# Larger VectorE steps, less work around the softmax, and a corner of wq loaded by four GpSimd DMAs

## The chip, the cores and the metric

One core of a Trainium2 chip runs the whole program. The metric is the device time of one execution in microseconds (us). Three executions of the kernel before took 1305.59, 1305.48 and 1307.32 us, median 1305.59 us. Weights, caches and activations lie in device memory (HBM); the core has 16 DMA engines that bring them into its on-chip memory (SBUF, 128 partitions), TensorE (PE) for matmuls into PSUM, VectorE (DVE), ScalarE (ACT), GpSimd (POOL) and SyncE (SP), which here only issues DMAs.

## The reference

A decode step of a transformer block, in float32, for 4 sequences (B) with one new token each, D = 512, H = 32 heads of Dh = 128, a cache of S = 4096 positions, F = 1792:

```python
xn = layernorm(x)
q = (xn @ wq) as [B, H, 1, Dh]
p = softmax((q . k_cache) * Dh ** -0.5)          # k_cache [B, H, S, Dh]
attention = (p . v_cache) as [B, 1, H*Dh] @ wo   # v_cache [B, H, S, Dh]
ffn = silu(xn @ w1) @ w2
out = x + attention + ffn
```

The two caches are 268 MB each, the weights wq and wo 8.4 MB each, w1 and w2 3.7 MB each. Every byte of them is read once.

## The kernel before

The work is cut into T = 32 tiles. One tile is one sequence and a group of G = 4 heads; its K and its V are 8.4 MB each, 64 KB in each of the 128 partitions: 32 partitions to a head, R = 128 positions to a partition. K tiles have two buffers (`kpool`, name `k_t`), V tiles one (`vpool`, name `v_t`). SP issues all loads in program order on one queue: w1, x, wq, K0, K1, and then V(i), K(i+2) in turn; the last V goes into a K buffer, and wo (two pieces) and w2 (four pieces of 7, 4, 2 and 1 rows of 2 KB a partition) come behind it. A load is issued when its buffer is free: for V(i) that is when the matmuls of V(i-1) are done, for K(i+2) when VectorE is done with K(i). The buffers of w1 and x (`scratch`) and wq (`wq_t`) are the first K buffer and the V buffer, so K1 waits for the feed-forward's first half and V0 for the projection of the queries.

Ahead of the tiles: layer norm on VectorE, `xn @ w1` and SiLU, `xn @ wq`, and a spread of q over partitions (`q_h`); `queries(n)` then makes, per four tiles, with four matmuls of 32 partitions, a copy of each head's q in all of the head's partitions.

For each tile, `products` multiplies K by q on VectorE (`STEP` = 32 positions at a time) and GpSimd adds the upper half of the products to the lower (`POOL_ROWS` positions, at the last step `POOL_ROWS_LAST`); `sums` reduces them on VectorE to scores; `maxima` finds a head's largest score; `softmax` on ScalarE writes exp(scale * s - scale * max) to `p_t`. `values` multiplies p by V on TensorE into `o_ps` (32 matmuls of 512 columns in four column groups), and `heads_out` takes from `o_ps` the block that belongs to each head: a ScalarE copy to `o_sb`, a VectorE multiplication by `own`, a VectorE reduction, and one matmul into `o_all`.

Behind the last tile: `heads_out` of tile 31, the division by the softmax sums (`o_row`), a transposition by matmuls (`ot`), the products with wo and the first 7 rows of w2 into `part`, a copy, the rest of w2 and the sums into `acc`, a copy to `res`, and four small stores. The order on each engine is that of the program as the scheduler leaves it; what a line waits for is set by the tiles it reads and writes.

Of the kernel before, what the change touches and what calls it, by code (L numbers as in the profile page):

```python
# [8 lines left out]
F32 = mybir.dt.float32  # L9
AF = mybir.ActivationFunctionType  # L10
ALU = mybir.AluOpType
AX = mybir.AxisListType.X

EPS = 1e-5
G = 4
STEP = 32
POOL_ROWS = 32
POOL_ROWS_LAST = 16
WO_CUTS = (16,)
W2_CUTS = (7, 11, 13)  # L20

# [2 lines left out]
def kernel(  # L24
# [23 lines left out]
    nc = tc.nc  # L48
    P = nc.NUM_PARTITIONS
    B, H, S, Dh = k_cache.shape  # L50
# [3 lines left out]
    FC = F // P  # L54
    FT = 4

    FN = [(FC + 3 - j) // 4 for j in range(4)]
    F0 = [sum(FN[:j]) for j in range(4)]
    PH = P // G
    R = S * G // P  # L60
    T = H // G * B
    NR = 4
    half = Dh // 2
    scale = float(Dh) ** -0.5
# [3 lines left out]
    const = ctx.enter_context(tc.tile_pool(name="const", bufs=1))  # L68
    kpool = ctx.enter_context(tc.tile_pool(name="kpool", bufs=2))
    vpool = ctx.enter_context(tc.tile_pool(name="vpool", bufs=1))  # L70
    small = ctx.enter_context(tc.tile_pool(name="small", bufs=2))
# [4 lines left out]
    def load_tile(pool, name, cache, i):  # L76
        t = pool.tile([P, R, Dh], F32, name=name)
        h, b = i // B * G, i % B
        src = cache[b, h : h + G].rearrange("h s d -> (h s) d")
        nc.sync.dma_start(t, src.rearrange("(p r) d -> p r d", p=P))  # L80
        return t
# [8 lines left out]
    nc.sync.dma_start(w1_t, w1.rearrange("(p c) f -> p c f", p=P))  # L90
    nc.sync.dma_start(x_sb, xf)
    wq_t = vpool.tile([P, R, Dh], F32, name="v_t").rearrange("p (c m) d -> p c (m d)", c=DC)
    nc.sync.dma_start(wq_t, wq.rearrange("(p c) n -> p c n", p=P))
    ks = {0: load_tile(kpool, "k_t", k_cache, 0)}


    const.tile([P, 48], F32, name="fill")
    ident = const.tile([P, P], F32, name="ident")
    make_identity(nc, ident)
    ones = const.tile([P, 1], F32, name="ones")  # L100
# [3 lines left out]
    p_t = const.tile([P, R, G], F32, name="p_t")  # L104
# [4 lines left out]
    m_t = const.tile([P, PH], F32, name="m_t")  # L109
# [13 lines left out]
    o_ps = ps_1.tile([P, NR * Dh], F32, name="o_ps")  # L123
    nc.vector.memset(o_ps, 0.0)
    acc = ps_1.tile([P, P], F32, name="acc")
    nc.vector.memset(acc, 0.0)
    o_all = ps_1.tile([H, B, Dh], F32, name="o_all")
    nc.tensor.matmul(
        o_all.rearrange("h b d -> h (b d)"), w_t[:, :H], p_t.rearrange("p r g -> p (r g)"),
        start=True, stop=False,  # L130
# [6 lines left out]
        axis=AX, op=ALU.add,  # L137
# [4 lines left out]
    own = const.tile([P, NR], F32, name="own")  # L142
# [4 lines left out]
    def accumulate(lhsT, rhs, start=False, stop=False):  # L147

        for j in range(D // P):
            nc.tensor.matmul(  # L150
                acc[32 * j : 32 * j + B, :], lhsT, rhs[:, j * P : (j + 1) * P],
                start=start, stop=stop,
            )

    accumulate(ident[:B, :B], x_sb, start=True)


# [32 lines left out]
    for c in range(DC):  # L190
        for j in range(4):
# [4 lines left out]
                start=(c == 0), stop=(c == DC - 1),  # L196
            )
    for j in range(4):
        rows, n = slice(32 * j, 32 * j + B), FN[j] * P
        nc.scalar.activation(h_sb[rows, :n], hp[rows, :n], AF.Silu)  # L200
    ht_ps = ps_s.tile([P, FT, 4, B], F32, name="sm")
    for t in range(FT):
# [3 lines left out]
            ident.rearrange("p (j m) -> p j m", j=4)[:, :, :B],  # L206
            start=True, stop=True,
        )
    ht_sb = const.tile([P, FT, 4, B], F32, name="ht_sb")
    nc.vector.tensor_copy(ht_sb, ht_ps)  # L210
    hT = [ht_sb[:, t, j, :] for j in range(4) for t in range(FN[j])]


    NM = H // G // 4
    qp = ps_s.tile([P, G * Dh], F32, name="sm")
    for m in range(NM):
        for c in range(DC):
            for j in range(4):
                n = NM * j + m
                a = PH - B - B * m  # L220
# [4 lines left out]
                    start=(m == 0 and c == 0),  # L225
                    stop=(m == NM - 1 and c == DC - 1),
# [5 lines left out]
    qh_ps = ps_q.tile([P, B, Dh], F32, name="q_ps")  # L232
    for b in range(B):
        for g in range(G):
# [4 lines left out]
                start=True, stop=True,  # L239
            )  # L240
    q_h = const.tile([P, B, Dh], F32, name="q_h")
    nc.vector.tensor_copy(q_h, qh_ps)  # L242

    q_ps, vs, st = {}, {}, {}

    def queries(n):

        t = ps_q.tile([P, B, Dh], F32, name="q_ps")
        for g in range(G):
            rows = slice(g * PH, (g + 1) * PH)  # L250
            k = g * PH + PH // 4 * (n // NM) + n % NM
            nc.tensor.matmul(  # L252
                t[rows].rearrange("p b d -> p (b d)"),
                ident[rows, k : k + 1].to_broadcast([PH, PH]),
                q_h[rows].rearrange("h b d -> h (b d)"),
                start=True, stop=True,
            )
        for b in range(B):
            q_ps[n * B + b] = t[:, b, :]

    def products(i, a):

        k, q = ks[i], q_ps[i]
        if a == 0:
            st[i] = small.tile([P, R], F32, name="s")
        z = a + STEP
        nc.vector.tensor_tensor(  # L267
            k[:, a:z, :], k[:, a:z, :], q[:, None, :].to_broadcast([P, STEP, Dh]), op=ALU.mult
        )
        v = a + halved(a)  # L270
        nc.gpsimd.tensor_tensor(  # L271
            k[:, a:v, :half], k[:, a:v, :half], k[:, a:v, half:], op=ALU.add
        )

    def halved(a):
        return POOL_ROWS if a + STEP < R else POOL_ROWS_LAST

    def sums(i, a):
        k, s = ks[i], st[i]
        v, z = a + halved(a), a + STEP  # L280
        if v < z:
            nc.vector.tensor_reduce(s[:, v:z], k[:, v:z, :], axis=AX, op=ALU.add)  # L282
        nc.vector.tensor_reduce(s[:, a:v], k[:, a:v, :half], axis=AX, op=ALU.add)  # L283

    def maxima(i):

        nc.vector.tensor_reduce(m_t[:, :1], st[i], axis=AX, op=ALU.max)  # L287
        mt = small.tile([P, PH], F32, name="mt", bufs=1)
        nc.vector.transpose(mt, m_t)
        gm = small.tile([P, 1], F32, name="gm", bufs=1)  # L290
        nc.vector.tensor_reduce(gm, mt, axis=AX, op=ALU.max)
        mb = small.tile([P, PH], F32, name="mb", bufs=1)
        nc.vector.tensor_scalar_mul(mb, gm.to_broadcast([P, PH]), -scale)
        nb = small.tile([P, PH], F32, name="nb", bufs=1)
        return nb, nc.vector.transpose(nb, mb).ins  # L295

    def softmax(i, nb):
        s = st.pop(i)
        for g in range(G):
            rows = slice(g * PH, (g + 1) * PH)  # L300
            nc.scalar.activation(  # L301
                p_t[rows, :, g], s[rows, :], AF.Exp, bias=nb[rows, :1], scale=scale,
                accum_out=l_t[rows, i % B, i // B, g : g + 1],
            )

# [15 lines left out]
    def heads_out(i):  # L321

        h, b = i // B * G, i % B
        o_sb = small.tile([P, NR, Dh], F32, name="o_sb", bufs=1)
        nc.scalar.activation(  # L325
            o_sb.rearrange("p r d -> p (r d)"), o_ps, AF.Copy
        )
        nc.vector.tensor_tensor(  # L328
            o_sb, o_sb, own[:, :, None].to_broadcast([P, NR, Dh]), op=ALU.mult
        )  # L330
        o_1 = small.tile([P, Dh], F32, name="o_1", bufs=1)
        nc.vector.tensor_reduce(o_1, o_sb.rearrange("p r d -> p d r"), axis=AX, op=ALU.add)  # L332
        nc.tensor.matmul(  # L333
            o_all[:, b, :], w_t[:, W0 - h : W0 - h + H], o_1, start=False, stop=(i == T - 1)
        )

    queries(0)
    ks[1] = load_tile(kpool, "k_t", k_cache, 1)
    nb = done = None
    for i in range(T):  # L340
# [12 lines left out]
        else:  # L353
            vs[i] = load_tile(kpool, "k_t", v_cache, i)
        for a in range(STEP, R, STEP):
            products(i, a)
            sums(i, a - STEP)
        sums(i, R - STEP)
        del ks[i], q_ps[i]
        nb, done = maxima(i)  # L360
# [5 lines left out]
    w2_t = kpool.tile([P, R, Dh], F32, name="k_t").rearrange("p r d -> p (r d)")  # L366
    w2_t = w2_t[:, : FC * D].rearrange("p (f n) -> p f n", f=FC)
    for t, w, n, cuts in ((wo_t, wo, H, WO_CUTS), (w2_t, w2, FC, W2_CUTS)):
        w = w.rearrange("(p f) n -> p f n", p=P)
        edges = (0, *cuts, n)  # L370
        for a, z in zip(edges[:-1], edges[1:]):
            nc.sync.dma_start(t[:, a:z, :], w[:, a:z, :])

    softmax(T - 1, nb)
    values(T - 1)
    heads_out(T - 1)


    ls_ps = ps_s.tile([H, B], F32, name="sm")
    for b in range(B):  # L380
        nc.tensor.matmul(
            ls_ps[:, b : b + 1], l_t[:, b].rearrange("p n g -> p (n g)"), ones,
            start=True, stop=True,
        )
    rl = const.tile([H, B], F32, name="rl")
    nc.vector.reciprocal(rl, ls_ps)
    o_row = const.tile([H, B, Dh], F32, name="o_row")
    nc.vector.tensor_tensor(
        o_row, o_all, rl[:, :, None].to_broadcast([H, B, Dh]), op=ALU.mult
    )  # L390
# [1 line left out]
    for n in range(NQ):  # L392
        nc.tensor.matmul(  # L393
            ot_ps, up[:, NQ - 1 - n : NQ - 1 - n + P], o_row[:, :, n * H : (n + 1) * H],
            start=(n == 0), stop=(n == NQ - 1),
        )
    ot = const.tile([P, H, B], F32, name="ot")
    nc.vector.tensor_copy(ot, ot_ps.rearrange("p b c -> p c b"))  # L398

    part = ps_q.tile([P, D], F32, name="q_ps")  # L400
    nc.vector.memset(part, 0.0)
    rows = [(ot[:, c, :], wo_t[:, c, :]) for c in range(H)]
    rows += [(hT[f], w2_t[:, f, :]) for f in range(W2_CUTS[0])]
    for c, (a, w) in enumerate(rows):
        j = 32 * (c % 4)
        nc.tensor.matmul(  # L406
# [3 lines left out]
    nc.scalar.activation(part_sb, part, AF.Copy)  # L410
    accumulate(pick[:, :B], part_sb)
    for f in range(W2_CUTS[0], FC):
        accumulate(hT[f], w2_t[:, f, :], stop=(f == FC - 1))

    res = small.tile([P, P], F32, name="s")
    nc.vector.tensor_copy(res, acc)  # L416
    for j in range(D // P):
        eng = nc.sync if j % 2 == 0 else nc.scalar
# [33 lines left out]
```

## Time and profile before

| what | us |
|---|---|
| median of three executions | 1305.59 |
| profiled execution, its time | 1305.64 |
| profiled execution, its span (first to last instruction) | 1303.9 |
| PE busy | 356.0 |
| VectorE busy | 973.8 |
| ScalarE busy | 92.7 |
| GpSimd busy | 511.2 |
| HBM read | 561.00 MB, 430 GB/s over the span |

The span is 1.74 us shorter than the execution's own time; that remainder lies outside the instructions. Times below count from the first instruction. A DMA that is spread over the 16 engines leaves sixteen landing events in the trace, one for each engine; from the first to the last of them one reads how far the engines have drifted apart. A packet record of the trace has its queue, start, duration and size; here a packet of 64 KB is one partition's row of one tile.

### The profile page before, as it was taken

The page shows a single profiled execution, that of the slowest core. Times are in us where ns is not written, and L with a number is a line of the kernel's source. Part 1 is how long each engine was busy: PE and PEld are TensorE (multiplying, and loading weights), DVE is VectorE, ACT ScalarE, POOL GpSimd, SP SyncE. Part 2 cuts the span into 40 slices and gives each one's busy share as a digit, 9 for nine tenths or more (in the row PEclk, how much of TensorE's full clock was granted, in tenths as well). Part 3 has the DMA queues.
Part 4 walks back from the last instruction along what each step waited for, and adds up shares of the span by engine and source line. Part 5 has one row for each costly group of instructions (what it writes and reads, how often), then busy time and mean ns, then how long its engine had stood idle before and what let it go on. Part 6 is the DMA issues. An engine that isn't in the chain of part 4 may idle for free.

```text
span 1303.9 us, 6301 instructions
## 1 busy us (share of the span) xinstructions
PE 356.0 (27%) x2484; PEld 88.1 (7%) x2484; DVE 973.8 (75%) x540; ACT 92.7 (7%) x297; POOL 511.2 (39%) x142
## 2 busy tenths in 40 slices
PE   4221223321222321133232033222113333112327
PEld 1000000000000000000000000000000000000002
DVE  1499777887777797777797777788777779777770
ACT  1010000000000000000000000000000000000000
POOL 0255333444333444332444433344433344433340
PEclk9755666655666665666665666665566665556668
DMA  9999999999999999999999999999999999999997
GB/s 402 449 420 447 422 445 424 443 426 442 427 439 431 436 433 434 434 433 435 435 431 439 430 437 430 439 428 441 426 438 429 438 429 440 427 442 427 441 423 330
DMA packets 10437, 561.40 MB, mean 431 GB/s; under 512 B 1172, under 2 KB 1188, under 8 KB 1448
## 3 DMA queue, kind: packets, MB, share of 16 engines
q1 hardware_dynamic: 10392, 561.01, 99.4%
q8 instruction: 19, 0.31, 0.1%
q14 instruction: 10, 0.08, 0.0%
q10 hardware_dynamic: 16, 0.00, 0.0%
HBM read 561.00 MB, written 0.01 MB: 430 GB/s over the span
## 4 chain that ended last, share of the span: by engine, by line
DMA 71%; PE 23%; another core or an unknown queue 4%; issue 2%; DVE 0%; ACT 0%; SPq 0%; ACTq 0%
DMA v_t<-in_A_v_cache_dram 65%; PE o_ps L312 21%; DMA k_t<-in_A_v_cache_dram 3%; DMA v_t<-in_A_wq_dram 2%; PE q_ps L406 1%; PE sm L221 1%; PE sm L393 0%; PE acc L150 0%; PE q_ps L235 0%; PE q_ps L252 0%; DVE o L332 0%; DVE o_sb L328 0%; DVE q_h L242 0%; DVE o_sb L231 0%
## 5 line engine op out<-in xcount | busy, mean ns | idle before, releaser
L271 POOL TENSOR_TENSOR k_t<-k_t 128x2048 f32<-128x2048 f32 (+1 forms) x128 | 508.9, 3986 | 745.8 <-DVE k_t L267 745.8
L267 DVE TENSOR_TENSOR k_t<-k_t,q_ps 128x4096 f32<-128x4096 f32 x128 | 562.3, 4414 | 224.6 <-DMA k_t<-in_A_k_cache_dram 224.6
L312 PE MATMUL o_ps<-v_t,p_t 128*16 128x512 f32 x1984 | 286.1, 741 | 826.2 <-DMA v_t<-in_A_v_cache_dram 826.2
L283 DVE TENSOR_REDUCE s<-k_t 128x32 f32<-128x2048 f32 (+1 forms) x128 | 257.7, 2013 | 12.0 <-POOL k_t L271 12.0
L312 PEld LDWEIGHTS o_ps<-v_t,p_t 128*16 128x16 f32 x1984 | 66.6, 113 | 1027.3 <-issue 948.3
L325 ACT ACTIVATE o_sb<-o_ps 128x512 f32<-128x512 f32 x32 | 19.1, 597 | 1097.1 <-issue 1081.1
L282 DVE TENSOR_REDUCE s<-k_t 128x16 f32<-128x2048 f32 x32 | 72.8, 2276 | 0.0
L301 ACT ACTIVATE p_t<-s,nb 32x128 f32<-32x128 f32 x128 | 66.5, 520 | 17.2 <-DVE nb L295 13.7
L328 DVE TENSOR_TENSOR o_sb<-o_sb,own 128x512 f32<-128x512 f32 x32 | 21.7, 678 | 27.8 <-ACT o_sb L325 27.7
L333 PE MATMUL o_all<-o,w_t 128*32 128x128 f32 x64 | 15.9, 338 | 88.4 <-DVE o L332 88.4
L332 DVE TENSOR_REDUCE o<-o_sb 128x128 f32<-128x512 f32 x32 | 32.7, 1023 | 3.2
L301 ACT ACTIVATION_READ_ACCUMULATOR p_t<-s,nb 32x1 f32 x128 | 25.5, 199 | 0.0
L333 PEld LDWEIGHTS o_all<-o,w_t 128*32 128x32 f32 x64 | 4.9, 119 | 117.8 <-DVE o L332 117.8
L312 PE MATMUL o_ps<-k_t,p_t 128*16 128x512 f32 x64 | 9.6, 765 | 7.2 <-DMA k_t<-in_A_v_cache_dram 7.2
L416 DVE COPY s<-acc 128x128 f32<-128x128 f32 x1 | 0.3, 292 | 12.9 <-PE acc L150 12.9
L287 DVE TENSOR_REDUCE m_t<-s 128x1 f32<-128x128 f32 x32 | 9.1, 285 | 1.1
L210 DVE COPY ht_sb<-sm 128x64 f32<-128x64 f32 x1 | 0.2, 225 | 12.7 <-PE sm L203 12.7
L295 DVE STREAM_TRANSPOSE nb<-mb 128x32 f32<-128x32 f32 x32 | 6.8, 212 | 3.3
L221 PE MATMUL sm<-v_t,xpad 128*32 128x512 f32 x64 | 8.6, 696 | 1.1 <-DMA v_t<-in_A_wq_dram 1.1
L252 PE MATMUL q_ps<-q_h,ident 32*32 32x512 f32 x64 | 8.5, 599 | 0.8 <-DVE q_h L242 0.8
L406 PE MATMUL q_ps<-v_t,ot 128*4 128x512 f32 x64 | 8.4, 683 | 0.4 <-DVE ot L398 0.4
L231 DVE COPY o_sb<-sm 128x512 f32<-128x512 f32 x1 | 0.7, 692 | 9.4 <-PE sm L221 9.4
(74 smaller groups left out, 73.3 us busy)
## 6 DMA issues: line engine op xcount, KB each, us to landing
v_t<-in_A_wo_dram SPq DMA_DIRECT2D x2, 4096.0 KB
k_t<-in_B_w_dram SPq DMA_DIRECT2D x1, 3584.0 KB, 11.2
k_t<-in_B_w_dram SPq DMA_DIRECT2D x1, 1792.0 KB, 33.0
k_t<-in_B_w_dram SPq DMA_DIRECT2D x1, 1024.0 KB, 35.0
k_t<-in_A_k_cache_dram SPq DMA_DIRECT2D x32, 48.3
k_t<-in_B_w_dram SPq DMA_DIRECT2D x1, 512.0 KB, 34.9
v_t<-in_A_v_cache_dram SPq DMA_DIRECT2D x31, 29.3
k_t<-in_B_w_dram SPq DMA_DIRECT2D x1, 256.0 KB, 35.1
```

What stands on the lines that cost most here:

```text
L221: nc.tensor.matmul(qp[32 * j : 32 * j + 32, :], xpad[:, c, a : a + PH], wq_t[:, c, n * G * Dh : (n + 1) * G * Dh], start=(m == 0 and c == ...
L267: nc.vector.tensor_tensor(k[:, a:z, :], k[:, a:z, :], q[:, None, :].to_broadcast([P, STEP, Dh]), op=ALU.mult)
L271: nc.gpsimd.tensor_tensor(k[:, a:v, :half], k[:, a:v, :half], k[:, a:v, half:], op=ALU.add)
L282: nc.vector.tensor_reduce(s[:, v:z], k[:, v:z, :], axis=AX, op=ALU.add)
L283: nc.vector.tensor_reduce(s[:, a:v], k[:, a:v, :half], axis=AX, op=ALU.add)
L301: nc.scalar.activation(p_t[rows, :, g], s[rows, :], AF.Exp, bias=nb[rows, :1], scale=scale, accum_out=l_t[rows, i % B, i // B, g : g + 1],)
L312: last = nc.tensor.matmul(o[j : j + NR * G, :], p_t[:, rows, :].rearrange("p r g -> p (r g)"), v[:, rows, :].rearrange("p r d -> p (r d)") ...
L325: nc.scalar.activation(o_sb.rearrange("p r d -> p (r d)"), o_ps, AF.Copy)
L328: nc.vector.tensor_tensor(o_sb, o_sb, own[:, :, None].to_broadcast([P, NR, Dh]), op=ALU.mult)
L332: nc.vector.tensor_reduce(o_1, o_sb.rearrange("p r d -> p d r"), axis=AX, op=ALU.add)
L333: nc.tensor.matmul(o_all[:, b, :], w_t[:, W0 - h : W0 - h + H], o_1, start=False, stop=(i == T - 1))
L406: nc.tensor.matmul(part[j : j + B, :], a, w, start=(c < 4), stop=(c >= len(rows) - 4))
```

## The change

- `STEP` goes from 32 to 64, `POOL_ROWS` to 64 and `POOL_ROWS_LAST` to 48, so a tile has two products, two GpSimd additions and three reductions in place of four, four and five. The same 16 positions of the last step are reduced whole by VectorE.
- The scale and the sign go into `q_h`, so that scores are negative and scaled; `maxima` then takes minima and needs no multiplication, and exp has scale -1.
- `queries` uses one matmul of 128 partitions against `spread`, a table that GpSimd makes from `ident` with two copies at the start.
- `heads_out`: for all tiles but the last the multiplication moves from VectorE to GpSimd, and the reduction becomes two GpSimd additions; for the last tile ScalarE's copy is left out, and VectorE multiplies straight from PSUM and adds twice.
- `hT` is copied with four copies in place of one; some buffers are shared; `acc` is cleared later.
- wq: SP loads the first 56 KB of each partition. The last 8 KB (WQ_TAIL = 2048 values) are loaded by four DMAs that GpSimd issues ahead of everything else on its queue: partitions 0 to 39 with the outer dimension 4 (ten rows each), 40 to 71 with 2 (sixteen each), 72 to 95 with 8 (three each) and 96 to 127 with 2 (sixteen each).

```diff
-STEP = 32
-POOL_ROWS = 32
-POOL_ROWS_LAST = 16
+STEP = 64
+POOL_ROWS = 64
+POOL_ROWS_LAST = 48
+WQ_TAIL = 2048
+WQ_SHARES = ((4, 40), (2, 32), (8, 24), (2, 32))
...
-    nc.sync.dma_start(wq_t, wq.rearrange("(p c) n -> p c n", p=P))
+    wq_f, src = wq_t.rearrange("p c n -> p (c n)"), wq.rearrange("(p c) n -> p (c n)", p=P)
+    cut = wq_f.shape[-1] - WQ_TAIL
+    nc.sync.dma_start(wq_f[:, :cut], src[:, :cut])
+    a = 0
+    for k, n in WQ_SHARES:
+        w = src[a : a + n, cut:].rearrange("(k q) n -> k q n", k=k)
+        nc.gpsimd.dma_start(wq_f[a : a + n, cut:], w)
+        a += n
...
-    ht_sb = const.tile([P, FT, 4, B], F32, name="ht_sb")
-    nc.vector.tensor_copy(ht_sb, ht_ps)
-    hT = [ht_sb[:, t, j, :] for j in range(4) for t in range(FN[j])]
+    hT = const.tile([P, FC, B], F32, name="hT")
+    for j in range(4):
+        z = F0[j] + FN[j]
+        nc.vector.tensor_copy(hT[:, F0[j] : z, :], ht_ps[:, : FN[j], j, :])
...
-    nc.vector.tensor_copy(q_h, qh_ps)
+    nc.vector.tensor_scalar_mul(q_h, qh_ps, -scale)
+    spread = const.tile([P, H // G, G, PH], F32, name="spread")
+    rows = ident.rearrange("p (g j m) -> p j g m", g=G, j=4)
+    for m in range(NM):
+        nc.gpsimd.tensor_copy(
+            spread.rearrange("p (j m) g i -> p m j g i", m=NM)[:, m],
+            rows[:, :, :, m, None].to_broadcast([P, 4, G, PH]),
+        )
...
-        for g in range(G):
-            rows = slice(g * PH, (g + 1) * PH)
-            k = g * PH + PH // 4 * (n // NM) + n % NM
-            nc.tensor.matmul(
-                t[rows].rearrange("p b d -> p (b d)"),
-                ident[rows, k : k + 1].to_broadcast([PH, PH]),
-                q_h[rows].rearrange("h b d -> h (b d)"),
-                start=True, stop=True,
-            )
+        nc.tensor.matmul(
+            t.rearrange("p b d -> p (b d)"),
+            spread[:, n].rearrange("p g i -> p (g i)"),
+            q_h.rearrange("h b d -> h (b d)"),
+            start=True, stop=True,
+        )
...
-        mb = small.tile([P, PH], F32, name="mb", bufs=1)
-        nc.vector.tensor_scalar_mul(mb, gm.to_broadcast([P, PH]), -scale)
-        return nb, nc.vector.transpose(nb, mb).ins
+        return nb, nc.vector.transpose(nb, gm.to_broadcast([P, PH])).ins
...
-        nc.scalar.activation(
-            o_sb.rearrange("p r d -> p (r d)"), o_ps, AF.Copy
-        )
-        nc.vector.tensor_tensor(
-            o_sb, o_sb, own[:, :, None].to_broadcast([P, NR, Dh]), op=ALU.mult
-        )
-        o_1 = small.tile([P, Dh], F32, name="o_1", bufs=1)
-        nc.vector.tensor_reduce(o_1, o_sb.rearrange("p r d -> p d r"), axis=AX, op=ALU.add)
+        if i < T - 1:
+            eng = nc.gpsimd
+            nc.scalar.activation(o_sb, o, AF.Copy)
+            eng.tensor_tensor(o_sb, o_sb, own_b, op=ALU.mult)
+        else:
+            eng = nc.vector
+            eng.tensor_tensor(o_sb, o, own_b, op=ALU.mult)
+        eng.tensor_tensor(o_sb[:, :2, :], o_sb[:, :2, :], o_sb[:, 2:, :], op=ALU.add)
+        o_1 = o_sb[:, 2, :]
+        eng.tensor_tensor(o_1, o_sb[:, 0, :], o_sb[:, 1, :], op=ALU.add)
```

More of the change, by code (lines that the diff above doesn't have):

```diff
@@ L92 @@
     wq_t = vpool.tile([P, R, Dh], F32, name="v_t").rearrange("p (c m) d -> p c (m d)", c=DC)
-    nc.sync.dma_start(wq_t, wq.rearrange("(p c) n -> p c n", p=P))
+    wq_f, src = wq_t.rearrange("p c n -> p (c n)"), wq.rearrange("(p c) n -> p (c n)", p=P)
[6 more added lines that the diff above has]
+        a += n
+    assert a == P
     ks = {0: load_tile(kpool, "k_t", k_cache, 0)}
-    const.tile([P, 48], F32, name="fill")
+    const.tile([P, 56], F32, name="fill")
     ident = const.tile([P, P], F32, name="ident")
@@ L125 @@
     acc = ps_1.tile([P, P], F32, name="acc")
-    nc.vector.memset(acc, 0.0)
     o_all = ps_1.tile([H, B, Dh], F32, name="o_all")
@@ L153, in accumulate @@
             )
+    nc.vector.memset(acc, 0.0)
     accumulate(ident[:B, :B], x_sb, start=True)
@@ L285, in maxima @@
     def maxima(i):
-        nc.vector.tensor_reduce(m_t[:, :1], st[i], axis=AX, op=ALU.max)
+        nc.vector.tensor_reduce(m_t[:, :1], st[i], axis=AX, op=ALU.min)
         mt = small.tile([P, PH], F32, name="mt", bufs=1)
@@ L290, in maxima @@
         gm = small.tile([P, 1], F32, name="gm", bufs=1)
-        nc.vector.tensor_reduce(gm, mt, axis=AX, op=ALU.max)
-        mb = small.tile([P, PH], F32, name="mb", bufs=1)
-        nc.vector.tensor_scalar_mul(mb, gm.to_broadcast([P, PH]), -scale)
+        nc.vector.tensor_reduce(gm, mt, axis=AX, op=ALU.min)
         nb = small.tile([P, PH], F32, name="nb", bufs=1)
-        return nb, nc.vector.transpose(nb, mb).ins
+        return nb, nc.vector.transpose(nb, gm.to_broadcast([P, PH])).ins
     def softmax(i, nb):
@@ L301, in softmax @@
             nc.scalar.activation(
-                p_t[rows, :, g], s[rows, :], AF.Exp, bias=nb[rows, :1], scale=scale,
+                p_t[rows, :, g], s[rows, :], AF.Exp, bias=nb[rows, :1], scale=-1.0,
                 accum_out=l_t[rows, i % B, i // B, g : g + 1],
@@ L324, in heads_out @@
         o_sb = small.tile([P, NR, Dh], F32, name="o_sb", bufs=1)
-        nc.scalar.activation(
-            o_sb.rearrange("p r d -> p (r d)"), o_ps, AF.Copy
-        )
-        nc.vector.tensor_tensor(
-            o_sb, o_sb, own[:, :, None].to_broadcast([P, NR, Dh]), op=ALU.mult
-        )
-        o_1 = small.tile([P, Dh], F32, name="o_1", bufs=1)
-        nc.vector.tensor_reduce(o_1, o_sb.rearrange("p r d -> p d r"), axis=AX, op=ALU.add)
+        o, own_b = o_ps.rearrange("p (r d) -> p r d", r=NR), own[:, :, None]
+        own_b = own_b.to_broadcast([P, NR, Dh])
+        if i < T - 1:
[8 more added lines that the diff above has]
+        eng.tensor_tensor(o_1, o_sb[:, 0, :], o_sb[:, 1, :], op=ALU.add)
         nc.tensor.matmul(
@@ L386 @@
     nc.vector.reciprocal(rl, ls_ps)
-    o_row = const.tile([H, B, Dh], F32, name="o_row")
+    o_row = small.tile([P, NR, Dh], F32, name="o_sb", bufs=1)[:H]
     nc.vector.tensor_tensor(
@@ L396 @@
         )
-    ot = const.tile([P, H, B], F32, name="ot")
+    ot = small.tile([P, P], F32, name="s").rearrange("p (c b) -> p c b", b=B)
     nc.vector.tensor_copy(ot, ot_ps.rearrange("p b c -> p c b"))
@@ L402 @@
     rows = [(ot[:, c, :], wo_t[:, c, :]) for c in range(H)]
-    rows += [(hT[f], w2_t[:, f, :]) for f in range(W2_CUTS[0])]
+    rows += [(hT[:, f, :], w2_t[:, f, :]) for f in range(W2_CUTS[0])]
     for c, (a, w) in enumerate(rows):
@@ L412 @@
     for f in range(W2_CUTS[0], FC):
-        accumulate(hT[f], w2_t[:, f, :], stop=(f == FC - 1))
+        accumulate(hT[:, f, :], w2_t[:, f, :], stop=(f == FC - 1))
     res = small.tile([P, P], F32, name="s")
```

## The prediction

> **What bounds the kernel now.** I read the page's slices and queues first, then the waits of SP's queue, the chain in order of time, the timeline of the end, and last the packet records and landing events.
>
> ```profile
> DMA  9999999999999999999999999999999999999997
> DMA packets 10437, 561.40 MB, mean 431 GB/s; under 512 B 1172, under 2 KB 1188, under 8 KB 1448
> q1 hardware_dynamic: 10392, 561.01, 99.4%
> q8 instruction: 19, 0.31, 0.1%
> q14 instruction: 10, 0.08, 0.0%
> ```
>
> The DMA engines never rest until the last slice. Nearly all packets come from SP's queue (q1); q8 and q14 fetch the engines' own instructions, 19 packets of 16 KB and 10 of 8 KB after the start.
>
> ```profile
> 1144.96 0.02 issue
> 1144.98 29.02 DMA v_t<-in_A_v_cache_dram
> 1174.00 0.04 issue
> 1174.04 8.98 PE o_ps L312 x64
> 1183.02 0.02 issue
> ```
>
> ```profile
> SPq L80 <- DMA v_t<-in_A_v_cache_dram: 830.0, 30, 29.8
> SPq L80 <- PE o_ps L312: 281.2, 30, 10.1
> SPq L80 <- DVE m_t L287: 36.5, 3, 28.1
> ```
>
> In the chain (start, duration, what) a V load lands, TensorE needs 9.0 us, the next V is issued. The 29 us of a load are 19.3 us of its own transfer behind the rest of a K transfer; both together take 38.6 us, 16.78 MB at 434 GB/s. V's issue thus has 10 us to spare, a K buffer (free about 28 us after its K landed, needed after 58) about 30. VectorE (30.4 us a tile) and GpSimd (15.9) are hidden under 38.6. So what sets the time is the number of bytes on the slowest of the 16 DMA engines, and the end behind V31:
>
> ```profile
> 1271.72 9.57 PE L312 MATMUL o_ps<-k_t,p_t 128*16 128x512 f32 x64 [7.21 <-DMA k_t<-in_A_v_cache_dram]
> ...
> 1281.42 0.60 ACT L325 ACTIVATE o_sb<-o_ps 128x512 f32<-128x512 f32 x1 [17.19 <-issue]
> 1282.05 0.69 DVE L328 TENSOR_TENSOR o_sb<-o_sb,own 128x512 f32<-128x512 f32 x1 [17.33 <-ACT o_sb L325]
> 1282.78 1.02 DVE L332 TENSOR_REDUCE o<-o_sb 128x128 f32<-128x512 f32 x1
> ...
> 1295.54 0.10 PEld L406 LDWEIGHTS q_ps<-k_t,ht_sb 128*4 128x4 f32 x4 [0.33 <-DMA k_t<-in_B_w_dram]
> ```
>
> A wait's time and releaser are in brackets. The landing events give what these lines do not. V31's sixteen come 0, .09, .17, .27, .53, .86, 2.04, 2.87, 2.94, 2.95, 3.07, 3.26, 3.31, 4.11, 4.33 and 4.53 us after the first; for w1, at 11 us, the spread is 0.76. The engines drift because instruction fetches take turns with data. In the packet records a 64 KB packet takes 2.418 us and starts 4 ns before the last one ends, and an 8 KB row of w2 takes 0.309. A 16 KB fetch takes 0.88 to 0.97, and the packet behind it 2.89 to 2.97: 1.43 us lost to that engine. The 19 return to the same engine after eight, so eight engines have two (2.86) or three (4.29). The count of 256 instructions to a fetch fits TensorE (4968). Of the 8 KB fetches, five (at 115, 377, 648, 919, 1191) cost 0.84 each, every seven tiles, which fits VectorE's rate: 4.2 on one engine. Three cost 0.55, two cost 0.53. That makes three groups: eight engines behind TensorE's fetches, four behind other fetches (.53, .86, 2.04, one above 4), four with none (0 to .27). V31 is complete when the latest engine is: 4.53 after the first.
>
> **The change part by part**, against the profiled execution's 1305.64 (span 1303.9; the median is 0.05 lower).
>
> *Tile work.* From the rows, a VectorE product of 4096 values takes 4.41 us and of 512 0.68: 0.144 + 1.042 per 1000. Products become 2 x 8.68 = 17.4. Reductions (2.28 for 2048, 1.21 for 1024) become 4.43 + 2.28 + 3.35 = 10.1, minima 0.285 + 0.212 + 0.186 + 0.212 = 0.9. That is 28.3 a tile in place of 30.4. GpSimd (4.53 for 2048, 2.37 for 1024: 2.1 ns a value) gets 8.8 + 6.7 + 1.3 + 0.8 + 0.5 = 18.1. Its second addition ends about 24.1 after a K's first product, where VectorE arrives at its last reduction (17.4 + 4.4 + 2.3 = 24.1): no wait of size. The K buffer is free at 28 as before. GpSimd waits in `heads_out` for ScalarE's copy, behind V(i-1)'s matmuls, about 30 us after K landed and 8.6 before the next; behind it stands only the next tile's addition. The matmul into `o_all` comes some 3 us after the copy, and TensorE has 10 us there. Cost nothing under 38.6 us; without that cover the saving would be 2 us a tile.
>
> *Start.* Four GpSimd DMAs stand ahead of `ident` and the clears. Not shown here; SP's issues take 0.36 to 0.40 each, its longest 0.57. Even 3 us each (12 in all) is before `ident` is needed (16.65) or nearly so. Meanwhile 10 to 16 rows of 8 KB (3.1 to 4.9 us) go between w1 and x, which lands that much after 11.99. So layer norm, `xn @ w1` and K1's issue (30.7) come up to 5 us later; K0's transfer covers K1 until 51, K1's covers V0 (issued 39.9) until 70. Products of tile 0 start at 51.5, q was ready at 43.7. Three more small VectorE copies (0.17 each) and two GpSimd copies go under the same. Cost nothing; it would need 15 us.
>
> *Instruction fetches.* VectorE executes 9 in place of 16 instructions a tile, so I expect three fetches in place of five by V31, 1.7 us off that engine. TensorE loses 96 of 4968 records: 28 us later, so the fetch at 1262.6 moves behind V31.
>
> *The balance.* Every engine loses eight times 8 KB of SP's rows: 8 x 0.302 = 2.42. The parts give their engines 10, 16 or 3 rows of 0.306: 3.06, 4.90, 0.92. Net +0.65 (four), +2.49 (two and two), -1.49 (eight). Which engine gets which part no trace of before shows. I take sixteen different ones, the 8-part on TensorE's eight, because 4 + 2 + 8 + 2 is 16 and the drift falls into the same groups, and x, a load of four partitions, lies on engines of the second group as far as I could follow them. Then V31's lags become 2.5 to 2.8 (no fetch), 1.2, 1.5, 2.7 and for VectorE's 0.05 + 2.5 + 0.65 = 3.2, and TensorE's eight 1.4 to 3.0. The latest is 3.2 in place of 4.53: -1.3.
>
> [...]
>
> *Changing queues.* A GpSimd row among SP's may cost more than its bytes. Low end 0: x's 2 KB packets on SP's own queue take 0.084 and the next 64 KB still 2.418. High end 0.53 a row: so much longer is the packet behind VectorE's 8 KB fetch; behind the other fetches it is 0.21 to 0.28. The nearest row by size is a fetch, but its excess goes with the target (five times 0.53, three times 0.24) and each comes alone; queued rows with the same kind of target are nearer to w2's. I take 0.03: 16 x 0.03 = +0.5 on the engines with sixteen rows, 3.3 in all, so about +0.2 to +0.5 on the latest. I count +0.5. The ends: 0, and 16 x 0.53 = +8.5 (latest 2.8 + 8.5 = 11.3).
>
> *The end.* ScalarE's copy goes: 0.63 with its handover. The reduction of 1.02 becomes additions of 0.41 + 0.28 with one more gap of 0.03: 0.3. So `ot` comes 0.92 earlier. But w2's first piece has landed on its last engine at 1295.23 and is used at 1295.54; V31 was used 0.05 after landing. So 0.25 is all that counts until the loads land earlier; the rest becomes a wait for wo's second piece and w2. With loads earlier by b the gain is the smaller of 0.92 + b and 0.25 + b.
>
> Sum: 1305.64 - 1.3 - 0.25 + 0.5 = 1304.6.
>
> **The rivals.**
> 1. *The rows cost double.* Each change of queue costs like the 8 KB fetches. At 0.24, the engines with sixteen rows lag .27 + 2.49 + 3.84 = 6.6 in place of 4.53: +2.1 - 0.25, 1307.5. At 0.53, +6.8 - 0.25, 1312. It turns to a loss at about 0.12 a row. For: every fetch shows an excess of at least 0.21. Against: the excess differs by target.
> 2. *The parts pile up or miss.* If each DMA begins at the same engine, two get 10 + 16 + 3 + 16 = 45 rows: 13.8 - 2.4 = +11.4, on a lag up to 3: 1314. If the 8-part misses TensorE's engines, a lag of 4.3 gets +2.5: 6.8, 1307.7.
> 3. *No rebalancing.* Each part is spread over all engines, nine rows at most in place of eight: +0.3 on a lag of 4.3 to 4.5, less 0.25: 1305.6. The drift speaks neither for nor against. [...]
> 4. *All engines end level.* The mean lag of 2.3 in place of 4.5, and 0.25: 1303.2, or 0.3 less with fewer fetches. That is the floor while bytes and rate stay.
>
> **How the numbers follow.** Forecast as summed (1303.6 to 1305.4) 0.52. Rival 1 below 0.2 a row (1305.4 to 1307) 0.13, above it 0.14, of which 0.08 end above 1308.2. Rival 2: 0.12, of which 0.09 above 1308.2. Rival 3: 0.06. Rival 4: 0.03. 0.2% (2.6 us) is about what a measurement of this kernel can tell from no change: below 1303.0 is faster, above 1308.2 slower. Faster 0.05 (rival 4 and a little of the forecast, with the spread of runs), slower 0.18 with 0.01 for what I did not see, same 0.77. The range 1303.2 to 1308.4 leaves out the pile-up and the dear rows.
>
> **What would show it.** Right: spread of V31's landings about 3 us, not 4.5; four GpSimd DMAs of 1 MB in all at the start; V31's matmuls start near 1270.9; no ScalarE copy behind them, and TensorE waiting inside L427's matmuls (wo, w2); VectorE's share near 70%. Wrong: packets longer than 0.309 us or followed by longer ones in the first 40 us, a spread above 4.5, a gap in the DMA row, or SP waiting for VectorE.

## The result and the profile after

The changed kernel takes 1312.67 us (median; 1312.05 to 1313.2), the kernel before in the same runs 1305.65. The ratio is 1.0054, 95% interval 1.0044 to 1.0065: slower by 7 us, where 1304.6 was forecast and 1308.4 was the upper end of the range. The profiled execution has a span of 1310.9 us against 1303.9.

The first lines are from the page of the kernel after: the DMA row of the forty slices, the packets, and the queues (packets, MB, share of 16 engines).

```profile
DMA  9999999999999999999999999999999999999998
GB/s 312 434 428 438 437 434 432 432 439 426 438 432 438 432 434 434 430 434 438 433 436 432 432 432 432 440 428 440 430 436 430 434 434 434 438 428 438 429 425 342
DMA packets 10644, 561.39 MB, mean 428 GB/s; under 512 B 1252, under 2 KB 1268, under 8 KB 1528
q1 hardware_dynamic: 10392, 559.96, 99.2%
q0 software_dynamic: 208, 1.05, 0.3%
q8 instruction: 19, 0.31, 0.1%
q14 instruction: 9, 0.07, 0.0%
```

The same row of before:

```profile
GB/s 402 449 420 447 422 445 424 443 426 442 427 439 431 436 433 434 434 433 435 435 431 439 430 437 430 439 428 441 426 438 429 438 429 440 427 442 427 441 423 330
```

The engines are as busy as before, yet the first slice moves 312 GB/s; before it was 402. The other slices lie between 420 and 449 in both, the last one apart. The new queue q0, GpSimd's, has the 1.05 MB of the tail in 208 packets, 13 for each of the 16 DMA engines: 128 rows of 8 KB and 80 packets of 4 bytes. A slice is 32.8 us, and 90 GB/s less in it are 2.9 MB, or 6.8 us of DMA time: nearly the whole loss is there.

The windows of before and then of after show the same (columns: window, its length, busy us of PE, weight loads, VectorE, ScalarE and GpSimd, granted clock, DMA share, GB/s).

```profile
0.00:20.00 20.00, 5.61 (x28) 1.53 (x32) 5.69 (x20) 1.49 (x2) 2.33 (x14) 1.00 0.95 394
20.00:40.00 20.00, 15.17 (x94) 4.76 (x86) 0.27 (x2) 3.42 (x5) 0.00 (x0) 0.83 1.00 433
```

```profile
0.00:20.00 20.00, 1.49 (x4) 0.29 (x4) 2.38 (x7) 1.28 (x1) 5.61 (x20) 1.00 0.97 306
20.00:40.00 20.00, 11.21 (x56) 3.78 (x55) 3.58 (x18) 3.62 (x6) 0.00 (x0) 0.82 0.99 360
40.00:60.00 20.00, 10.79 (x98) 3.49 (x98) 2.04 (x3) 0.00 (x0) 0.00 (x0) 0.84 1.02 440
```

For 35 us the engines count as busy and move a fifth less. Behind that everything is late by a constant: the timeline has the first product, released by K0, at 59.34 in place of 51.52 (before, then after).

```profile
51.52 8.75 DVE L267 TENSOR_TENSOR k_t<-k_t,q_ps 128x4096 f32<-128x4096 f32 x2 [8.95 <-DMA k_t<-in_A_k_cache_dram]
59.34 17.29 DVE L285 TENSOR_TENSOR k_t<-k_t,q_ps 128x8192 f32<-128x8192 f32 x2 [8.08 <-DMA k_t<-in_A_k_cache_dram]
```

From there on the kernel behaves as before. SP's waits are the same (V's landing 829.1 us, TensorE 278.1), and the V loads of the chain follow each other at 38.7 us on average, as before:

```profile
SPq L82 <- DMA v_t<-in_A_v_cache_dram: 829.1, 30, 29.5
SPq L82 <- PE o_ps L329: 278.1, 30, 10.1
SPq L82 <- DVE m_t L306: 37.1, 2, 28.1
```

The end of after, from the timeline of TensorE, is what the prediction had for it: no ScalarE copy behind V31's matmuls, and waits for wo's second piece (1.08) and w2's first (0.64) inside the last products.

```profile
1279.18 8.51 PE L329 MATMUL o_ps<-k_t,p_t 128*16 128x512 f32 x64 [5.75 <-DMA k_t<-in_A_v_cache_dram]
1289.40 0.41 PE L354 MATMUL o_all<-o_sb,w_t 128*32 128x128 f32 x2 [1.71 <-DVE o_sb L353]
...
1298.50 3.62 PE L427 MATMUL q_ps<-v_t,s 128*4 128x512 f32 x32 [1.08 <-DMA v_t<-in_A_wo_dram]
1302.76 1.89 PE L427 MATMUL q_ps<-k_t,hT 128*4 128x512 f32 x14 [0.64 <-DMA k_t<-in_B_w_dram]
```

The packet records say where the 7 us are. On each engine they form one chain without gaps; while q0 has work, one packet of q0 comes between two of SP's, and most of them take longer. I followed the sixteen chains from packet to packet. The GpSimd rows are not 10, 16 or 3 to an engine. About 9 are on twelve engines, and 7, 5, 4 and 4 on the others; that is what ranges of 3, 2, 2 and 2 partitions to an engine give for DMAs of 40, 32, 24 and 32 partitions. Engines with 4 or 5 rows finish wq at 37.0 to 37.3, the others at 38.0 to 39.4: nearly as late. So the first suspects were the number of q0's packets, equal for all engines (theory V: 7.5 us / 13 = 0.58 each), and the placement (theory P, which supposes that each part's rows now go through other engines than those that carry the same partitions in the 128-partition loads, and meet those on the way into SBUF; the records show 9, 7, 5 or 4 rows of the tail on an engine and eight of the 56 KB packets). A third, C, is that something else of the change costs it.

### The profile page after: what moved, and what is told of

Same layout as the page of the kernel before. It is cut to its first block, busy times and chain, and to the rows that moved or that the text cites. A ratio compares the mean times of both kernels' runs of the same rounds, so it can differ in the third digit from the quotient of the medians.

```text
span 1310.9 us, 6011 instructions
## 1 busy us (share of the span) xinstructions
PE 353.0 (27%) x2436; PEld 88.4 (7%) x2436; DVE 911.1 (69%) x322; ACT 91.8 (7%) x296; POOL 571.7 (44%) x177
## 3 DMA queue, kind: packets, MB, share of 16 engines
q0 software_dynamic: 208, 1.05, 0.3%
## 4 chain that ended last, share of the span: by engine, by line
DMA 76%; PE 23%; issue 0%; SPq 0%; ACT 0%; DVE 0%; ACTq 0%; DVEq 0%
DMA v_t<-in_A_v_cache_dram 71%; PE o_ps L329 22%; DMA v_t<-in_A_wq_dram 3%; DMA k_t<-in_B_w_dram 2%; PE sm L233 1%; PE acc L161 0%; PE q_ps L427 0%; SPq L393 0%; ACT o_sb L431 0%; SPq L92 0%; SPq L93 0%; DVE s L437 0%; ACTq L431 0%; DVEq L437 0%
## 5 line engine op out<-in xcount | busy, mean ns | idle before, releaser
L285 DVE TENSOR_TENSOR k_t<-k_t,q_ps 128x8192 f32<-128x8192 f32 x64 | 553.1, 8683 | 295.7 <-DMA k_t<-in_A_k_cache_dram 295.7
L289 POOL TENSOR_TENSOR k_t<-k_t 128x4096 f32<-128x4096 f32 x64 | 497.4, 7796 | 543.6 <-DVE k_t L285 543.6
L301 DVE TENSOR_REDUCE s<-k_t 128x64 f32<-128x4096 f32 x64 | 248.7, 3886 | 14.4 <-POOL k_t L289 12.6
L347 POOL TENSOR_TENSOR o_sb<-o_sb,own 128x512 f32<-128x512 f32 x31 | 32.2, 1039 | 151.4 <-ACT o_sb L346 151.4
L354 PE MATMUL o_all<-o_sb,w_t 128*32 128x128 f32 x64 | 15.9, 340 | 99.3 <-POOL o_sb L353 97.6
L351 POOL TENSOR_TENSOR o_sb<-o_sb 128x256 f32<-128x256 f32 x31 | 22.4, 722 | 2.4
L353 POOL TENSOR_TENSOR o_sb<-o_sb 128x128 f32<-128x128 f32 x31 | 14.1, 454 | 2.4
L354 PEld LDWEIGHTS o_all<-o_sb,w_t 128*32 128x32 f32 x64 | 5.0, 121 | 128.1 <-POOL o_sb L353 125.5
L427 PE MATMUL q_ps<-v_t,s 128*4 128x512 f32 x64 | 8.9, 709 | 1.5 <-DMA v_t<-in_A_wo_dram 1.1
L312 DVE STREAM_TRANSPOSE nb<-gm 128x32 f32<-128x32 f32 x32 | 6.8, 212 | 3.7 <-DVE gm L310 0.5
```

Of the source, the lines that this page charges most:

```text
L285: nc.vector.tensor_tensor(k[:, a:z, :], k[:, a:z, :], q[:, None, :].to_broadcast([P, STEP, Dh]), op=ALU.mult)
L289: nc.gpsimd.tensor_tensor(k[:, a:v, :half], k[:, a:v, :half], k[:, a:v, half:], op=ALU.add)
L347: eng.tensor_tensor(o_sb, o_sb, own_b, op=ALU.mult)
L351: eng.tensor_tensor(o_sb[:, :2, :], o_sb[:, :2, :], o_sb[:, 2:, :], op=ALU.add)
L353: eng.tensor_tensor(o_1, o_sb[:, 0, :], o_sb[:, 1, :], op=ALU.add)
L354: nc.tensor.matmul(o_all[:, b, :], w_t[:, W0 - h : W0 - h + H], o_1, start=False, stop=(i == T - 1))
```

## The experiments

### Which half of the change: all of wq on SP, and only the four DMAs

The first kernel is the changed one without the split of wq:

```diff
-    nc.sync.dma_start(wq_f[:, :cut], src[:, :cut])
-    a = 0
-    for k, n in WQ_SHARES:
-        w = src[a : a + n, cut:].rearrange("(k q) n -> k q n", k=k)
-        nc.gpsimd.dma_start(wq_f[a : a + n, cut:], w)
-        a += n
-    assert a == P
+    nc.sync.dma_start(wq_t, wq.rearrange("(p c) n -> p c n", p=P))
```

> The changed kernel with all of wq in one load on SP's queue, as before; the four GpSimd DMAs are gone and every other edit stays. Theory V (each descriptor of a second queue that comes between SP's packets costs its DMA engine about 0.58 us beyond its bytes: 13 of them on each engine, 7.5 us) and theory P (rows that an engine writes to partitions it does not otherwise serve hold up other engines): the delay is in the GpSimd DMAs, so K0 lands near 51.5 us as before and the time is 1305.65 - 0.25 (the end) - up to 0.3 (fewer fetches), 1305.0 to 1305.5. Theory C (the larger steps, the later clears or the GpSimd work in heads_out cost it): still about 1312.

Measured: 1305.58 us (1305.0 to 1305.89) against 1305.57 of before, ratio 0.9999 (0.9989 to 1.0008). The second is the kernel before with the split and the loop of after added, and nothing else.

> The kernel before with only the four GpSimd DMAs added for the last 8 KB a partition of wq. V and P: K0 lands at about 59 us, 1312.5 to 1313.5, about 7 us over the kernel before. C: 1305.4 to 1306.

Measured: 1313.34 us, ratio 1.0057 (1.004 to 1.0074). The four DMAs are the whole loss, and the other edits are worth nothing that can be measured. C falls. The end of e1's profile shows why they gain so little:

```profile
1285.43 5.31 PE L421 MATMUL q_ps<-v_t,s 128*4 128x512 f32 x32 [0.38 <-DVE s L413]
1291.05 3.62 PE L421 MATMUL q_ps<-v_t,s 128*4 128x512 f32 x32 [0.30 <-DMA v_t<-in_A_wo_dram]
1295.30 1.89 PE L421 MATMUL q_ps<-k_t,hT 128*4 128x512 f32 x14 [0.64 <-DMA k_t<-in_B_w_dram]
```

Its products with w2 start at 1295.30, before they had started at 1295.54 (weight load): `ot` is ready earlier, and TensorE waits for the loads instead. The span is 1303.4 in place of 1303.9, a difference too small for the timing to tell from nothing.

### A second queue without other placement: one DMA of 128 partitions

```diff
-    for k, n in WQ_SHARES:
-        w = src[a : a + n, cut:].rearrange("(k q) n -> k q n", k=k)
-        nc.gpsimd.dma_start(wq_f[a : a + n, cut:], w)
-        a += n
-    assert a == P
+    nc.gpsimd.dma_start(wq_f[:, cut:], src[:, cut:])
```

and the same with `nc.scalar.dma_start`.

> The changed kernel with the last 8 KB a partition of wq in one GpSimd DMA of 128 partitions: eight rows on each engine, placed as SP places its own rows, and one completion descriptor, so 9 descriptors of the second queue an engine in place of 13. V: 9 x 0.58 = 5.2 us, 1310 to 1311. P: no row is on another engine than before, so about what e1 gives, 1305 to 1306. Uneven rows as the cause (engines with nine rows): same as P.

> As e3, but the one DMA of 128 partitions is issued by ScalarE on its hardware queue. V with any second queue: 5.2 us, 1310 to 1311. V with the cost in GpSimd's queue alone (descriptors made by software): 1305 to 1306. P: 1305 to 1306.

Measured: 1305.58 us with GpSimd's queue (ratio 0.9998, 0.9989 to 1.0007), 1305.2 with ScalarE's (0.9997, 0.9988 to 1.0006). V falls: nine packets of a second queue on every engine (q0 of e3 has 144 in all), one by one between SP's, cost nothing. In e3's records the rows take 0.310 us each and all 128 packets of 56 KB 2.116, as if they were alone (in after, those of 35 us and later, behind the last row, take 2.116 too). The windows of e3 have nearly the bandwidth of before (394 and 433 GB/s):

```profile
0.00:20.00 20.00, 3.19 (x18) 0.90 (x22) 5.59 (x20) 1.49 (x2) 4.09 (x17) 1.00 0.96 394
20.00:40.00 20.00, 16.35 (x88) 4.87 (x92) 0.41 (x4) 3.42 (x5) 0.00 (x0) 0.83 0.98 423
```

### Placement, evenness, number of DMAs, bytes

Four kernels part these. The first has no second queue:

```diff
-    for k, n in WQ_SHARES:
-        w = src[a : a + n, cut:].rearrange("(k q) n -> k q n", k=k)
-        nc.gpsimd.dma_start(wq_f[a : a + n, cut:], w)
-        a += n
-    assert a == P
+    for a in (0, P // 2):
+        nc.sync.dma_start(wq_f[a : a + P // 2, cut:], src[a : a + P // 2, cut:])
```

> The changed kernel without any GpSimd or ScalarE load: SP loads the first 56 KB a partition of wq in one DMA and the last 8 KB in two more DMAs on its own queue, partitions 0 to 63 and 64 to 127. One queue, even rows. Theory P (what costs is that a DMA of fewer than 128 partitions puts rows on other engines than the 128-partition loads do, so that several engines meet at the same partitions): slower than e1 (1305.58), by at least 1 and at most the 7.4 us of the changed kernel. Theory N (the number of DMAs of a second queue, and the completion descriptors that each leaves on every engine): 1305.6. Theory U (nine rows here, four there): 1305.6. [...]

The second has the loop of after with even parts:

```diff
-WQ_SHARES = ((4, 40), (2, 32), (8, 24), (2, 32))
+WQ_SHARES = ((16, 32), (16, 32), (16, 32), (16, 32))
```

> The changed kernel with the four GpSimd DMAs of 32 partitions each: every engine gets two rows of each, eight in all, as in a 128-partition load, but mostly rows of other partitions. P: slower than e1 by 2 to 7 us, 1307.5 to 1312.7. U (the uneven 9, 7, 5, 4 rows): 1305.6. N: about as the changed kernel, 1312.7. [...]

The third cuts the tail by columns, so that each of the four DMAs has all partitions:

```diff
-    for k, n in WQ_SHARES:
-        w = src[a : a + n, cut:].rearrange("(k q) n -> k q n", k=k)
-        nc.gpsimd.dma_start(wq_f[a : a + n, cut:], w)
-        a += n
-    assert a == P
+    n = WQ_TAIL // 4
+    for a in range(cut, cut + WQ_TAIL, n):
+        nc.gpsimd.dma_start(wq_f[:, a : a + n], src[:, a : a + n])
```

> The changed kernel with the last 8 KB in four GpSimd DMAs of all 128 partitions and 2 KB a partition each: as many DMAs and completion descriptors as the change has, 32 rows of 2 KB an engine that change queues, but every row on the engine that serves its partition anyway. P and U: 1305.5 to 1306.2 (descriptor overhead of some 10 ns a row, 0.3 us). N: 1311 to 1314.

The fourth is after with `WQ_TAIL = 1024` in place of 2048:

> The changed kernel with half the bytes in the four GpSimd DMAs (the last 4 KB a partition), same partitions, same number of rows. P, cost by bytes that meet: about half the loss, 1308 to 1310. N, or any cost by row: the loss stays, 1312 to 1313.

| kernel | us | ratio to before (95% interval) |
|---|---|---|
| e5, two DMAs of 64 partitions on SP's queue | 1308.28 | 1.0021 (1.0011 to 1.0031) |
| e6, four GpSimd DMAs of 32 partitions | 1312.76 | 1.0055 (1.004 to 1.007) |
| e7, four GpSimd DMAs of 128 partitions | 1305.65 | 1.0 (0.9991 to 1.001) |
| e8, after with half the bytes | 1309.35 | 1.0027 (1.0015 to 1.0039) |

Even parts do not help (e6 is as slow as after), four DMAs in place of one do not hurt (e7), half the bytes cost half (e8: 3.8 of 7), and two DMAs of 64 partitions, on SP's own queue alone, cost 2.7 us (e5). All four agree with P. e6 alone does not part P from N: 1312.76 is the upper end of P's range and is also where N had it. e7 is what rules N out. Its q0 has 320 packets with 1.05 MB, 64 of them under 512 B; the other 256 are 4.1 KB in the mean, where 512 rows of 2 KB were expected. The 10 ns a row in that expectation were an estimate: a 2 KB packet of x took 0.084 us in before, where 1/32 of a 64 KB packet (2.418) is 0.076.

The packet records give the sizes, mean us of one packet:

| | 28 KB of w1 | 56 KB of wq | 8 KB of the tail |
|---|---|---|---|
| e3, one DMA of 128 partitions | 1.164 | 2.116 | 0.310 |
| e5, two of 64 on SP | 1.165 | 2.120 | 0.602 |
| e6, four of 32 on GpSimd | 1.468 | 2.544 | 0.446 |
| after | 1.412 | 2.687 | 0.412 |

In e5 sixteen engines write to half of the partitions (q1 has 160 packets more than in e1: 128 rows, and 32 under 512 B, sixteen to a DMA), and a row takes twice as long: 8 x (0.602 - 0.310) = 2.3 us an engine, against 2.7 measured. The first packet of K0 on each engine, right behind the tail, is slow too: 3.16 us on average in place of 2.418. In after, an engine's eight packets of each kind lose 8 x 0.248 + 8 x 0.571, and its eight rows on average 8 x 0.102: 7.4 us, and K0's first product is 7.2 later than in e3 (59.34 against 52.17, the line below). So the loss is mostly not in the 1 MB that was moved, but in SP's packets, which are slowed while GpSimd's rows are under way.

```profile
52.17 17.28 DVE L280 TENSOR_TENSOR k_t<-k_t,q_ps 128x8192 f32<-128x8192 f32 x2 [7.49 <-DMA k_t<-in_A_k_cache_dram]
```

No engine is spared. In e6 the last tail row ends at 31.07 us, and all 85 packets of 56 KB that start before that take 2.22 us or more; the 32 that start after 32 us take 2.12. A tail row on the engine itself is not needed: between 15 and 27 us of after, a 56 KB packet right behind a tail row takes 2.88 us on average, and one behind another packet 2.95. The records do not tell a packet's partition, so they cannot say whether a slowed packet goes to the partitions of the tail rows. That rows meet on the way into SBUF is therefore argued, from the doubling in e5, and not shown; a part also reads from a smaller stretch of wq than a load of 128 partitions, and no run separates the reading from the writing.

In the first two windows of e5, the 20 to 40 us have the loss, where the tail comes; in e6, like after, both:

```profile
0.00:20.00 20.00, 5.50 (x28) 1.54 (x32) 5.69 (x20) 1.49 (x2) 3.35 (x16) 1.00 0.98 408
20.00:40.00 20.00, 15.40 (x94) 4.29 (x86) 0.67 (x5) 3.42 (x5) 0.00 (x0) 0.91 0.98 353
```

```profile
0.00:20.00 20.00, 1.98 (x4) 0.29 (x4) 2.85 (x7) 1.28 (x1) 5.50 (x20) 1.00 0.98 304
20.00:40.00 20.00, 11.85 (x59) 4.10 (x62) 3.11 (x17) 3.62 (x6) 0.00 (x0) 0.84 0.98 374
```

### Why e6 costs 7 us and e5 only 2.7

e6's four parts on SP's queue, behind the 56 KB:

```diff
-    for k, n in WQ_SHARES:
-        w = src[a : a + n, cut:].rearrange("(k q) n -> k q n", k=k)
-        nc.gpsimd.dma_start(wq_f[a : a + n, cut:], w)
-        a += n
-    assert a == P
+    for a in range(0, P, 32):
+        nc.sync.dma_start(wq_f[a : a + 32, cut:], src[a : a + 32, cut:])
```

> As e6 (four DMAs of 32 partitions each for the last 8 KB of wq), but on SP's own queue behind the first 56 KB. If rows on other engines cost only among themselves: 2.4 to 3 us as in e5, 1308 to 1308.6. If such rows cost more because they meet the rows of a second queue (e6: 7.2 us), this one stays near e5. If four parts are worse than two by themselves: 1310 or more.

Measured: 1308.21 us, ratio 1.0019 (1.0009 to 1.0028). The same four parts cost 2.6 us behind SP's packets and 7.2 among them. The reading that fits: on one queue the rows of a part meet only each other and the edges of their neighbours. On a second queue they are spread over some 26 us of SP's packets (5.6 to 31.1 us in e6) and hold up packets of 28 and 56 KB, 3.5 and 7 times as large as a row (1.468 and 2.544 us in e6, 1.164 and 2.116 in e3). How they do it is open, and parts on ScalarE's queue, which would tell whether it takes GpSimd's queue, were not tried.

### What became of the 4, 2, 8 and 2 parts

```diff
-        nc.gpsimd.dma_start(wq_f[a : a + n, cut:], w)
+        nc.sync.dma_start(wq_f[a : a + n, cut:], w)
```

> The changed kernel with its four partial loads, in the same 4, 2, 8 and 2 parts of the same partitions, issued by SP on its own queue behind the first 56 KB. If the outer dimension decides there how many engines carry a part, each part beginning at the same engine, two engines get 10 + 16 + 3 + 16 = 45 rows of 8 KB (13.8 us at 0.306, up to twice that where they meet others), and the time is 1305.6 - 2.4 + 13.8 = 1317 or more. If it is spread over all sixteen engines, as GpSimd's queue did: about what e10 gives, 1308.2 to 1309. If it fell on sixteen different engines, as the prediction had it for GpSimd: 1304 to 1307.

Measured: 1309.95 us, ratio 1.0032 (1.002 to 1.0043). None of the three cases fits to the letter. The four DMAs leave 10, 16, 12 and 16 landing events, where the outer dimensions are 4, 2, 8 and 2. The rows per engine that I could follow are about 10 on ten engines, 6 on two and 4 on four; that is 40 partitions on ten engines (4 each), 32 on sixteen (2 each), 24 on twelve (2 each) and 32 on sixteen (2 each). A row takes 0.713 us on average, longer than in e10 (0.552). So on this queue, too, the engines went with the number of partitions (40 on ten, 32 on sixteen, 24 on twelve), and the outer dimension of 4, 2, 8 and 2 is not seen in them. The split `(k q) n -> k q n` leaves the rows in the order they had; the two dimensions are one run of evenly spaced rows, and nothing of the split is seen in where the rows went. On GpSimd's queue the same DMAs were spread differently: the counts of after fit 3, 2, 2 and 2 partitions to an engine.

### The end of the kernel

From e1: `W2_CUTS = (5, 9, 12)` in place of `(7, 11, 13)`.

> e1 (the changed kernel with all of wq on SP) with the pieces of w2 cut at rows 5, 9, 12 in place of 7, 11, 13, so that what TensorE waits for ahead of its last stretch is smaller and lands two rows of 256 KB (1.2 us) earlier. In e1 TensorE idles 0.30 us for wo's second piece and 0.64 us for w2's first. Reading that the end hangs on the landings and not on the compute behind V31: up to 0.5 us faster than e1 (until the last piece's landing binds), 1305.0 to 1305.4. Reading that the end hangs on the compute: the same or slower, 1305.6 to 1306.

Measured: 1305.67 us, ratio 0.9999 (0.999 to 1.0008). It is inconclusive. In its profiled execution TensorE's products behind V31 took 9.79 us, in e1's 9.29, and the transposition 2.07 against 1.15, so `ot` came 1.6 us later and the waits that the cut was to shorten were not there. No kernel of this study was measurably faster than the kernel before.

## Why the prediction was wrong

- **What bounds the kernel:** right. The bytes of the DMA engines and the end behind them set the time; K0's first product is 7.2 us later than in e3, and at the end the kernel is 7.1 us behind e3 and e1 (1312.67 against 1305.58).
- **Tile work hidden:** right. VectorE falls from 973.8 to 911.1 us (28.5 a tile; 28.3 in the prediction), GpSimd rises to 571.7 (17.9; 18.1), and e1 is at 1305.58.
- **Start:** right in that nothing of the arithmetic came on the path: x released its first reduction at 18.39 (6.4 later; up to 5 was said), V0 was issued at 48.64 in place of 39.94, still before K1 had landed. Wrong in what it did not ask: whether the transfers themselves keep their rate.
- **The balance:** this is the step that failed. Its term was -1.3 us; the split of wq made +7.1 (1312.67 against 1305.58 in e1, the same kernel without it). It took each part to be on engines of its own, with 10, 16 or 3 rows to an engine by the outer dimension; no run shows these rows. The trace has the rows on all sixteen engines, 9, 7, 5 or 4 each, which fits 3, 2, 2 and 2 partitions to an engine, and in e11, on SP's queue, the outer dimension is not seen either (10, 16, 12 and 16 engines). The second half of the step, that 8 KB cost 0.306 us wherever they go, failed with it and is the one that cost the time: 0.41 us for the row itself, and 0.25 (28 KB) to 0.57 us (56 KB) more for each of SP's packets meanwhile. Why those packets are slowed is open. The spread of V31's landings was 5.27 us, not 3.
- **Changing queues:** right about what it asked, and nearer to zero than the 0.03 that it took: e3 and e7 cost nothing. Rival 1, which would have given 1307.5 to 1312, comes near the measured time by luck: it had the change of queue as the cause.
- **Rival 3** had the rows right (nine at most) and its time wrong, 1305.6: it priced the uneven rows and not the loads of fewer partitions, of which two in e5 were 2.7 us dearer than one load.
- **Instruction fetches:** the small ones fell from ten to nine in all, TensorE's stayed at 19, the eighteenth now behind V31 (1275.8 us in e1), and e1's spread for V31 is 4.6 as before: seventeen fetches come ahead of it, so one engine still has three, and in e1 one engine lands 1.2 us after all the others. The sum had counted that only together with the balance.
- **The end:** -0.25 was small and fits e1's span (-0.5); the timing can't tell it from nothing.

Not tried: a load that really gives single engines more rows. On both queues the engines of a part went with its number of partitions (after, e11), and every load in parts of fewer than 128 partitions that was tried cost 2.6 us or more besides (e5, e6, e8, e10, e11). Whether the drift of 4.5 us could be evened out is therefore open.

## What to carry to other kernels

Where the DMA engines are the bound, load all 128 partitions in each DMA and cut along the free dimension. Here cutting 1 MB by partitions cost 2.6 to 4.3 us behind the other loads (e5, e10, e11) and 7 us among them; cutting it by columns cost nothing, from GpSimd's queue (e3 1305.58, e7 1305.65) or ScalarE's (e4 1305.2). The DMA row's busy share hides the loss, as a slowed packet counts as busy for as long as it takes: it is 0.97 and 0.99 in the first two windows of after, with 306 and 360 GB/s. GB/s by slice or window shows it. Before a sum counts on which engine gets which row, look at the landing events or packet records of a load of that shape; the shape as written in the program need not be what decides.

## What the runs showed that I had not expected

- A packet of SP's queue takes 2.69 us in place of 2.12 (56 KB, mean of after) while another queue loads parts of 24 to 40 partitions, though an engine carries only 4 to 9 of their rows; with rows of DMAs of 128 partitions beside it (e3, e7) it stays at 2.12.
- Sixteen engines writing 64 partitions need 0.602 us for a row of 8 KB, writing 128 partitions 0.310; writing 32 partitions (e10) 0.552 on average, no more than with 64.
- The same DMA of 40 partitions went to ten engines from SP's queue (ten landing events); from GpSimd's the rows counted on each engine fit fourteen.
